# Attention and two mixture layers in one Trainium2 kernel: a new written order of the steps that hold both attention and the first layer's matmuls

## The chip, the cores and the metric

The kernel runs on one core of one Trainium2 chip. The metric is device time in microseconds (us), from several runs; one further execution was taken with the hardware profiler, and all rows of the trace come from that one. Engines are named as in the profile: PE (TensorE matmul), PEld (its weight load), DVE (VectorE), ACT (ScalarE), POOL (GpSimd), SP (SyncE, which here only issues DMAs).

## The reference, cut to what matters

```python
scores = scale * q @ k.T            # 4 batches, 8 heads, 576 positions, head size 64
scores += bias (ALiBi); causal window of 128
attn = softmax(scores) @ v          # -> x, 2304 tokens x 512
a, b = x @ w_a, x @ w_b             # 512 -> 1536
x = (a * b) @ w_out                 # 1536 -> 512
logits = x @ w_gate + modality_bias[modality_id]
e_idx = argmax(logits); gate_w = softmax(logits)[e_idx]      # 8 experts
out = gate_w * (relu(x @ w1[e_idx]) @ w2[e_idx])             # 512 -> 1024 -> 512
```

## The kernel before, in words

The 2304 tokens are 18 tiles of 128. They are worked in seven chunks of 3, 2, 2, 3, 3, 3 and 2 tiles (chunks 0 to 6). For each chunk there are twelve steps j, one for each block of 128 columns of w_a and w_b. The loop `for c ... for j` at L1149 calls `step0` for chunk 0 and `step` for chunks 1 to 5; chunk 6 has a loop body of its own (L1183 on).

**A step on PE.** `mm_ab(c, j, 0)` (12 matmuls, product "a"), `mm_ab(c, j, 1)` (product "b"), then pieces of attention, then `mm_out` (L539, L535), which adds the output product of the step before. Values are held as a high and a low half (type fp32r), so each product is three matmuls.

**Attention beside it.** One item is one query tile of a pair of heads. It takes three steps: in the first `score_mm` (PE), the mask and maximum on DVE (`score_sel`, `score_max`), `score_exp` on ACT; in the second the sum's inverse on DVE, `score_nrm` on ACT (L300), the transposes `pt_tr` on PE (L317) and `pt_cp`, which copies the high half on ACT (L330), subtracts the low half on DVE (L331) and masks twice on POOL into `pt` (L333, L335); in the third `a_pv`, the product with V ("PV", L401), two copies `u` out of PSUM on ACT (L408), two small DMAs to `z` and an addition on POOL; `z_add` adds `z` a step later. Items run ahead of their chunk: while chunk c is in its steps, attention of chunk c+1 is computed. `x_split` at the end of a chunk makes the next chunk's two halves `xr`. In `step` the list `sc` holds the items of the second stage, `tp` those of the third, `new` those that begin. In chunk 0 the PV of chunk 1's items goes through `pv_mm`, `pv_ev`, a transpose `pv_tr` (L369) and a copy `pv_x`.

**The gated product.** `gf` = a*b on DVE (L1102, needs the copy `asb` of a by ACT), its high half `g` on ACT (L1115), its low half on DVE (L1116). `mm_out` of the next step reads both; for the last step of a chunk `mm_out` stands right at the start of the next chunk.

**Routing.** `evac_out` copies a chunk's finished sums on ACT (L635) into tiles `x2`, of which there are three. For chunks 2 to 5 the logits are made on DVE (`rd_dot`, L620, one dot per tile and expert in steps 1 to 8), and then each tile has a generator in the list `ranks`: its first part is the argmax and the exponential, its second the gate value (`gate`, which also issues the DMA of `x2` to the table `x2d`, L580), the rank by two small matmuls, and a scatter. Before, the first part of at most two tiles runs in a step and the second part of one tile at the end of a step: for three tiles, the second parts end steps 9, 10 and 11. Chunks 0 and 1 go through `route` and the list `tr`.

**Output weights.** They come as float64 (`wo_load`, L484, into `wor`), are turned into float32 by three DVE instructions (`wo_jobs(j-1)` in step j of chunk 0, tile `f64o`) and written to DRAM as `wo_f` (L495). `wor`, `f64o` and the later `wo` share one tag "wo" with four buffers.

**What sets the order.** From chunk 0's steps to the end of chunk 5 the orders of PE, ACT and DVE are those of the program text (manual schedule); SP and POOL, and all of chunk 6, are ordered by the scheduler.

Of the kernel before, what the change touches and what calls it, by code (L numbers as in the profile page):

```python
# [16 lines left out]
P = 128  # L17
# [4 lines left out]
def attn_moe_moe2(ctx: ExitStack, tc, q, k, v, moe_w_a, moe_w_b, moe_w_out, modality_id,  # L22
# [33 lines left out]
    const = ctx.enter_context(tc.tile_pool(name="const", bufs=1))  # L56
    rt = ctx.enter_context(tc.tile_pool(name="rt", bufs=2))
    m1 = ctx.enter_context(tc.tile_pool(name="m1", bufs=2))
# [327 lines left out]
    def a_pv(it):  # L386
        a, t = it.a, it.t
        xf_new(a)
        if a.c in V32:
            pv_mm(it)  # L390
            pv_ev(it)
            pv_tr(it)
            pv_x(it, 0)
            return

        ps = ps_at.tile([P, 4, P], F32, tag="att", name="ps_o")
        for h in range(2):
            for b in range(2):  # L400
                nc.tensor.matmul(ps[:, 1 - h::2], lhsT=a.vv[:, t + b, h].rearrange("p r d -> p (r d)"),  # L401
                                 rhs=it.pt[:, h, b], start=(b == 0), stop=(b == 1))
        u = at.tile([P, 3, P], F32, tag="u", bufs=2, name="u")
        z = at.tile([P, P], F32, tag="z", bufs=2, name="z")
        n = slice(t * P, (t + 1) * P)
        for h in range(2):
            o = 64 * h
            nc.scalar.copy(out=u[o:o + 64], in_=ps[o:o + 64, 1 - h:4 - h])  # L408
# [3 lines left out]
        nc.gpsimd.tensor_tensor(out=xf_t[a.c, a.hp][:, n], in0=u[:, 0], in1=u[:, 2], op=ALU.add)  # L412
        zq.append(lambda: nc.gpsimd.tensor_tensor(out=xf_t[a.c, a.hp][:, n], in0=xf_t[a.c, a.hp][:, n],
                                                  in1=z, op=ALU.add))

    def z_add():
        for f in zq:
            if "pt" in mark:
                with tc.issue_after(mark["pt"]):
                    f()  # L420
            else:
                f()
        zq.clear()
# [140 lines left out]
    def route_fin(i, t, x2, pl, late=False):  # L564
# [20 lines left out]
        nc.vector.tensor_scalar(out=oh, in0=iot[:, 0:E], scalar1=sc[:, 2:3], scalar2=None, op0=ALU.is_equal)  # L585
        yield
        if t is None:
            pr = ps_at.tile([P, E], F32, tag="att", name="ps_r")
        else:
            pr = ps_acc.tile([P, E], F32, tag=f"acc{t}", name="ps_r")  # L590
        nc.tensor.matmul(pr, lhsT=tri, rhs=oh, start=True, stop=False)
        nc.tensor.matmul(pr, lhsT=ones, rhs=osum, start=False, stop=True)
        if late:
            gate()
        nc.vector.tensor_tensor(out=osum, in0=osum, in1=oh, op=ALU.add)
# [413 lines left out]
    def step0(j, pend, sc, tp):  # L1009

        n, last = CH[0] * P, j == NJ - 1
        new = list(range(cur["s"], goal[j]))
        its = [live[g] for g in tp]
        if j + 2 < NJ:
# [31 lines left out]
        for f in js[3:4]:  # L1046
            f()
        for it in its:
            pv_tr(it)
            pv_x(it, 0)  # L1050
        for g in new:
            score_red(live[g])
        if last:
            wo_fetch(0, 1)
            wo_fetch(1, 1)
            x_split(1)
        for g in new:
# [436 lines left out]
```

## Time and profile before

| | us |
|---|---|
| runs before, median (lowest to highest) of 3 | 854.33 (854.24 to 855.41) |
| the profiled execution, its own time | 853.42 |
| its span, first to last instruction | 851.4 |
| mean granted clock of PE in it | 0.988 |

The page of the profile gives the busy time of each engine over the span, then slices, the longest groups and the chain that ended last. Chunk 0's steps lie at about 46 to 142 us, chunk 1 to 219, chunk 2 to 295, chunk 3 to 380, chunk 4 to 473, chunk 5 to 560, chunk 6 to about 615; then come the experts. In a timeline row the first number is the start in us, the second the length; what stands in brackets at the end is the idle time of the engine just before and what ended it. A group of several instructions in one row ("x2") may hold short gaps.

### The profile page before, as it was taken

How to read it: one execution, taken by the hardware profiler on the slowest of the kernel's cores; microseconds unless marked ns; L12 is line 12 of the kernel's file. 1: busy time of each engine (PE TensorE's matmuls, PEld its weight loads, DVE VectorE, ACT ScalarE, POOL GpSimd, SP SyncE). 2: the span in 40 equal slices, each digit the busy share in tenths (PEclk: the TensorE clock that was granted, in tenths of full speed). 3: DMA queues.
4: the chain of work that ended last, by engine and by line, in shares of the span. 5: the costliest groups of instructions: out<-in, count | busy, mean ns of one | idle time of the engine just before them, and what ended most of it. 6: DMA issues, size and time to landing. Idle time of an engine off the chain costs nothing.

```text
span 851.4 us, 14429 instructions
## 1 busy us (share of the span) xinstructions
PE 810.0 (95%) x4726; PEld 727.2 (85%) x4726; DVE 541.2 (64%) x1559; ACT 458.4 (54%) x1149; POOL 230.1 (27%) x349
## 2 busy tenths in 40 slices
PE   7898999999999999999999899999999999999994
PEld 5876777898888899999999799988988998989893
DVE  7668887777666676667776667567575544448320
ACT  6743435777777776677666643322345443547420
POOL 5411000343234333352324322201132130114011
PEclk9899999999999999999999999999999999999998
DMA  8993325577556696554555444358438655448301
GB/s 242 370 388 105 105 95 176 178 210 225 178 145 169 167 218 165 152 149 141 164 148 154 105 131 127 106 150 269 132 122 284 222 174 154 149 143 289 122 32 39
DMA packets 77348, 144.60 MB, mean 170 GB/s; under 512 B 13839, under 2 KB 40623, under 8 KB 77264
## 3 DMA queue, kind: packets, MB, share of 16 engines
q1 hardware_dynamic: 73712, 133.86, 52.2%
q0 software_dynamic: 3552, 9.73, 3.1%
q8 instruction: 39, 0.64, 0.3%
q14 instruction: 45, 0.37, 0.1%
HBM read 118.16 MB, written 22.12 MB: 165 GB/s over the span
## 4 chain that ended last, share of the span: by engine, by line
PE 68%; ACT 8%; DMA 8%; DVE 7%; issue 6%; POOL 2%; SPq 1%; POOLq 0%; ACTq 0%; DVEq 0%
PE ps_ab L522 27%; PE acc L539 11%; PE ps_y L1230 9%; PE ps_h L1247 8%; PE acc L535 3%; PE ps_o L401 2%; DMA x2d<-x 2%; PE ps_s L253 2%; ACT u L408 2%; PE ps_p L317 1%; PE ps_o L356 1%; ACT p L277 1%; DVE g L1116 1%; DMA xg<-x2d,idx 1%; PE ps_t L970 1%
## 5 line engine op out<-in xcount | busy, mean ns | idle before, releaser
L522 PE MATMUL ps_ab<-xr,wab 128*128 128x384 f32 (+1 forms) x2016 | 323.8, 316 | 3.1 <-ACT asb L1196 1.6
L522 PEld LDWEIGHTS ps_ab<-xr,wab 128*128 128x128 f32 x2016 | 306.9, 188 | 12.8 <-issue 4.5
L539 PE MATMUL acc<-wo,g 128*128 128x512 f32 x540 | 138.7, 398 | 1.6 <-ACT g L1115 1.6
L333 POOL TENSOR_SCALAR_AFFINE_SELECT pt<-pc 128x512 fp32r<-128x512 f32 (+1 forms) x72 | 43.8, 608 | 305.1 <-DVE pc L331 217.6
L539 PEld LDWEIGHTS acc<-wo,g 128*128 128x128 f32 x540 | 97.7, 190 | 20.6 <-ACT g L1115 2.4
L1247 PE MATMUL ps_h<-xT,w1s 128*128 128x384 f32 x576 | 104.3, 337 | 0.0
L1230 PE MATMUL ps_y<-w2s,h 128*128 128x512 f32 x432 | 104.1, 394 | 0.0
L1247 PEld LDWEIGHTS ps_h<-xT,w1s 128*128 128x128 f32 x576 | 99.7, 188 | 1.4 <-issue 0.5
L1230 PEld LDWEIGHTS ps_y<-w2s,h 128*128 128x128 f32 x432 | 79.8, 188 | 15.8
L277 ACT ACTIVATE p<-p,mx 128x128 f32<-128x128 f32 x144 | 56.7, 395 | 48.5 <-DVE mx L267 48.1
L620 DVE CUSTOM_DVE_ANT_0 junk<-x,wgt 128x512 f32<-128x512 f32 x88 | 62.1, 705 | 8.3 <-DMA wgt<-in_wgt 3.6
L1116 DVE TENSOR_TENSOR g<-gf,g 128x384 fp32r<-128x384 f32 (+1 forms) x60 | 40.6, 676 | 33.3 <-ACT g L1115 32.9
L408 ACT COPY u<-ps_o 64x384 f32<-64x384 f32 x104 | 49.3, 474 | 9.4 <-PE ps_o L401 6.6
L921 DVE TENSOR_TENSOR w2s<-wr,w2s 128x1024 fp32r<-128x1024 f32 x24 | 29.4, 1225 | 38.3 <-ACT w2s L920 38.0
L1102 DVE TENSOR_TENSOR gf<-ps_ab,asb 128x384 f32<-128x384 f32 (+1 forms) x60 | 30.2, 503 | 36.5 <-PE ps_p L317 20.4
L1237 POOL DMA_INDIRECT out<-y,idx x18 | 21.5, 1194 | 113.6 <-ACT y L1236 111.8
L300 ACT ACTIVATE p<-p,mx 128x128 f32<-128x128 f32 x104 | 36.2, 395 | 24.8 <-DVE mx L285 24.6
L1250 ACT ACTIVATE h<-ps_h 128x384 fp32r<-128x384 f32 x48 | 23.5, 490 | 44.1 <-PE ps_h L1247 44.0
L921 DVE TENSOR_TENSOR w1s<-wr,w1s 128x1024 fp32r<-128x1024 f32 x28 | 34.3, 1224 | 20.4 <-ACT w1s L920 20.4
L335 POOL TENSOR_SCALAR_AFFINE_SELECT pt<-pc 128x512 fp32r<-128x512 f32 (+1 forms) x72 | 46.4, 645 | 0.0
L1251 DVE SCALAR_TENSOR_TENSOR h<-ps_h,h 128x384 fp32r<-128x384 f32 x48 | 26.4, 554 | 27.7 <-ACT h L1250 27.7
L317 PE MATMUL ps_p<-ident,p 128*128 128x128 f32 x144 | 32.3, 290 | 10.5 <-ACT p L300 10.0
(221 smaller groups left out, 1207.2 us busy)
## 6 DMA issues: line engine op xcount, KB each, us to landing
wo<-wo_d SPq DMA_DIRECT2D x60, 512.0 KB, 3.9
wr<-in_moe_w SPq DMA_DIRECT2D x56, 512.0 KB, 4.5
wgt<-in_wgt SPq DMA_DIRECT2D x32, 256.0 KB, 3.4
wraw<-in_moe_w_a SPq DMA_DIRECT2D x12, 512.0 KB, 8.6
wraw<-in_moe_w_b SPq DMA_DIRECT2D x12, 512.0 KB, 9.3
wor<-in_moe_w_out SPq DMA_DIRECT2D x12, 512.0 KB, 3.6
wo_d<-wo SPq DMA_DIRECT2D x12, 512.0 KB, 3.3
kr<-in_k SPq DMA_DIRECT2D x24, 256.0 KB, 4.0
```

What stands on the lines that cost most here:

```text
L277: nc.scalar.activation(out=it.p[:, h, :], in_=it.p[:, h, :], func=AF.Exp, bias=it.mx[:, 2 + h:3 + h], scale=-1.0, accum_out=it.mx[:, 4 + h ...
L317: nc.tensor.transpose(it.pp[:, h, :], it.p[:, h, :], ident)
L333: nc.gpsimd.affine_select(out=it.pt[:, :, 0], in_=pc, pattern=pat + [[-1, P]], base=0, channel_multiplier=1, compare_op=ALU.is_gt, fill=0.0)
L335: mark["pt"] = nc.gpsimd.affine_select(out=it.pt[:, :, 1], in_=pc, pattern=pat + [[1, P]], base=0, channel_multiplier=-1, compare_op=ALU.i ...
L408: nc.scalar.copy(out=u[o:o + 64], in_=ps[o:o + 64, 1 - h:4 - h])
L522: nc.tensor.matmul(ps[:, :n], lhsT=w[:, m, r, kk * P:(kk + 1) * P], rhs=xr[:, s, kk, :n], start=(idx == 0), stop=(idx == len(terms) - 1))
L539: nc.tensor.matmul(acc[c, t], lhsT=g[:, r, t * P:(t + 1) * P], rhs=w[:, s, :], start=(j == 0 and idx == 0), stop=(j == NJ - 1 and idx == 2))
L620: nc.vector.tensor_tensor_reduce(out=junk, in0=x2[:, 0:DM], in1=wgt[0][:, e % 2], scale=1.0, scalar=0.0, op0=ALU.mult, op1=ALU.add, accum_ ...
L921: nc.vector.tensor_tensor(out=dst[:, 1], in0=srcw, in1=dst[:, 0], op=ALU.subtract)
L1116: nc.vector.tensor_tensor(out=gt[:, 1, :n], in0=gf[:, :n], in1=gt[:, 0, :n], op=ALU.subtract)
L1230: nc.tensor.matmul(pss[t], lhsT=h[:, r, f, t * P:(t + 1) * P], rhs=W2[f // 2][:, s_, f % 2, :], start=(f == 0 and i == 0), stop=(f == 7 an ...
L1247: nc.tensor.matmul(ps, lhsT=W1[f // 2][:, r, kk, (f % 2) * P:(f % 2 + 1) * P], rhs=xT[:, s_, kk, :], start=(kk == 0 and i == 0), stop=(kk ...
```

## The change

(1) `rt` has three buffers instead of two. (2) `a_pv` now holds the PV matmuls alone, and the copies, DMAs and additions are a function `pv_out`; in `step`, PV stands right behind product b and ahead of `pt_tr`. (3) In `step`, `g`'s high half and low half stand right behind `gf`, ahead of `pt_cp` and of the copies `u` on ACT and ahead of L331 and `score_sel` on DVE. (4) In `step0` the items of the third stage have `pv_tr` and `pv_x` behind `mm_out`, and so have the last step's `wo_fetch` and `x_split(1)`; step 0 has no PV any more, step 1 does it for two items. (5) The late form of `route_fin` has its gate as a part of its own; in `step` all tiles of `ranks` take their first part in one step and their gate in the next, and one tile takes its last part at the end of a step from there on. (6) `wo_load(j)` is called in step j from step 1 on, in place of `wo_load(j+1)`. (7) A check that all `z` of a chunk are added before `x_split`.

```diff
-    rt = ctx.enter_context(tc.tile_pool(name="rt", bufs=2))
+    rt = ctx.enter_context(tc.tile_pool(name="rt", bufs=3))
...
     def a_pv(it):
         a, t = it.a, it.t
         xf_new(a)
...
-        ps = ps_at.tile([P, 4, P], F32, tag="att", name="ps_o")
+        it.po = ps_at.tile([P, 4, P], F32, tag="att", name="ps_o")
         for h in range(2):
             for b in range(2):
-                nc.tensor.matmul(ps[:, 1 - h::2], lhsT=a.vv[:, t + b, h].rearrange("p r d -> p (r d)"),
+                nc.tensor.matmul(it.po[:, 1 - h::2], lhsT=a.vv[:, t + b, h].rearrange("p r d -> p (r d)"),
                                  rhs=it.pt[:, h, b], start=(b == 0), stop=(b == 1))
+
+    def pv_out(it):
...
         yield
+        if late:
+            gate()
+            yield
         if t is None:
...
-        if late:
-            gate()
             pr = ps_at.tile([P, E], F32, tag="att", name="ps_r")
...
-        its = [live[g] for g in tp]
+        its = [live[g] for g in tp] if j else []
...
-        for it in its:
-            pv_tr(it)
-            pv_x(it, 0)
         for g in new:
             score_red(live[g])
-        if last:
-            wo_fetch(0, 1)
-            wo_fetch(1, 1)
-            x_split(1)
         for g in new:
             score_exp(live[g])
         new_preps(goal[j + 2], goal[j])
         if pend is not None:
             mm_out(*pend, wo_t[j - 1])
+        for it in its:
+            pv_tr(it)
+            pv_x(it, 0)
+        if last:
+            wo_fetch(0, 1)
+            wo_fetch(1, 1)
+            x_split(1)
...
-        return (0, j, gf), new, sc
+        return (0, j, gf), new, sc if j else tp + sc
...
-        for r in ranks[:2]:
-            if r[0] == 0:
+        for r in ranks:
+            if r[0] < 2:
                 next(r[1])
-                r[0] = 1
+                r[0] += 1
...
+        gt = m1.tile([P, 2, MT * P], F32R, tag="g", bufs=2, name="g")
+        nc.scalar.copy(out=gt[:, 0, :n], in_=gf[:, :n])
+        nc.vector.tensor_tensor(out=gt[:, 1, :n], in0=gf[:, :n], in1=gt[:, 0, :n], op=ALU.subtract)
+        for g in tp:
+            a_pv(live[g])
         for g in sc:
             pt_tr(live[g])
             pt_cp(live[g])
         z_add()
         for g in tp:
-            a_pv(live.pop(g))
+            pv_out(live.pop(g))
         for g in new:
             c_, hp_, t_ = items[g]
             live[g] = score_mm(pairs[c_, hp_], t_)
         for g in new[:1]:
             score_sel(live[g])
-        gt = m1.tile([P, 2, MT * P], F32R, tag="g", bufs=2, name="g")
-        nc.scalar.copy(out=gt[:, 0, :n], in_=gf[:, :n])
-        nc.vector.tensor_tensor(out=gt[:, 1, :n], in0=gf[:, :n], in1=gt[:, 0, :n], op=ALU.subtract)
...
-        if ranks and ranks[0][0] == 1:
+        if ranks and ranks[0][0] == 2:
             next(ranks.pop(0)[1], None)
...
-                if j + 1 < NJ:
-                    wo_load(j + 1)
+                if j:
+                    wo_load(j)
```

## Rows read from the trace of the kernel before

**Rows 1.** Windows: length; busy PE, PEld, DVE, ACT, POOL; granted clock, DMA, GB/s.

```profile
46.00:150.00 104.00, 97.46 (x485) 77.68 (x484) 82.93 (x159) 42.69 (x113) 11.83 (x20) 1.00 0.49 165
150.00:219.00 69.00, 65.28 (x471) 59.07 (x469) 49.40 (x165) 51.95 (x146) 26.45 (x41) 1.00 0.67 207
219.00:295.00 76.00, 71.30 (x507) 64.31 (x507) 48.44 (x166) 54.68 (x155) 28.46 (x49) 1.00 0.58 158
295.00:475.00 180.00, 180.00 (x1052) 168.99 (x1051) 130.72 (x440) 121.49 (x325) 65.08 (x103) 1.00 0.61 161
```

**Rows 2.** Waits of PE: us in total, times, longest.

```profile
PE ps_p L317 <- ACT p L300: 10.0, 11, 3.3
...
PE ps_o L369 <- ACT u L362: 1.9, 3, 0.7
...
PE acc L539 <- ACT g L1115: 1.6, 2, 1.0
```

**Rows 3.** Timeline of PE in chunk 0.

```profile
67.52 2.84 PE L535 MATMUL acc<-f64o,gf 128*128 128x512 f32 x6 [3.55 <-DVE f64o L446]
```

**Rows 4.** Timeline of DVE in chunk 0.

```profile
63.80 0.52 DVE L442 TENSOR_SCALAR f64o<-wor 128x512 uint32<-128x512 uint32 x1 [4.97 <-DMA wo_f<-f64o]
```

**Rows 5.** The page, DMA issues: size, median us to landing.

```profile
wor<-in_moe_w_out SPq DMA_DIRECT2D x12, 512.0 KB, 3.6
```

**Rows 6.** Timeline of PE in chunk 2, transposes of two steps.

```profile
227.75 0.62 PE L317 MATMUL ps_p<-ident,p 128*128 128x128 f32 x2 [0.28 <-ACT p L300]
...
289.75 0.62 PE L317 MATMUL ps_p<-ident,p 128*128 128x128 f32 x2 [0.19 <-ACT p L300]
```

**Rows 7.** Timeline of ACT in chunk 2, one step.

```profile
242.09 0.38 ACT L330 CAST pc<-ps_p 128x256 fp32r<-128x256 f32 x1
...
243.34 0.41 ACT L1115 CAST g<-gf 128x256 fp32r<-128x256 f32 x1
244.74 0.41 ACT L277 ACTIVATE p<-p,mx 128x128 f32<-128x128 f32 x1 [0.99 <-DVE mx L267]
```

**Rows 8.** Timeline of DVE in chunk 2, the same step.

```profile
242.49 0.42 DVE L331 TENSOR_TENSOR pc<-ps_p,pc 128x256 fp32r<-128x256 f32 x1 [0.26 <-ACT pc L330]
242.83 0.42 DVE L261 COPY_PREDICATED ps_s<-upper,ps_s 128x256 f32<-128x256 uint8 x1
243.78 0.71 DVE L1116 TENSOR_TENSOR g<-gf,g 128x256 fp32r<-128x256 f32 x1 [0.53 <-ACT g L1115]
```

**Rows 9.** Timelines of SP's queue and of ACT between chunks 4 and 5.

```profile
474.13 0.38 SPq L580 DMA_DIRECT2D x2d<-x  x1
...
480.37 0.59 ACT L635 COPY x<-acc 128x512 f32<-128x512 f32 x1 [3.11 <-DMA x2d<-x]
```

**Rows 10.** Timeline of PE, second step of chunk 5.

```profile
486.51 0.77 PE L317 MATMUL ps_p<-ident,p 128*128 128x128 f32 x2 [3.34 <-ACT p L300]
```

**Rows 11.** Windows, the same stretch: columns as in the first group.

```profile
486.00:493.00 7.00, 6.49 (x22) 5.51 (x23) 6.10 (x19) 4.46 (x13) 2.42 (x4) 0.53 0.16 48
```

**Rows 12.** Timelines of ACT and of PE at the start of chunk 6.

```profile
565.75 0.58 ACT L635 COPY x<-acc 128x512 f32<-128x512 f32 x1 [2.63 <-DMA x2d<-x]
...
566.66 3.12 PE L522 MATMUL ps_ab<-xr,wab 128*128 128x256 f32 x24 [1.59 <-ACT asb L1196]
```

**Rows 13.** Timelines of ACT, DVE and PE, a step of chunk 4.

```profile
406.25 0.70 ACT L300 ACTIVATE p<-p,mx 128x128 f32<-128x128 f32 x2 [0.50 <-DVE mx L285]
...
409.01 0.37 ACT L330 CAST pc<-ps_p 128x256 fp32r<-128x256 f32 x1 [1.04 <-PE ps_p L317]
...
410.44 0.51 ACT L1115 CAST g<-gf 128x384 fp32r<-128x384 f32 x1
...
409.57 0.55 DVE L1102 TENSOR_TENSOR gf<-ps_ab,asb 128x384 f32<-128x384 f32 x1
...
408.54 0.38 PE L317 MATMUL ps_p<-ident,p 128*128 128x128 f32 x2
408.68 0.72 PE L401 MATMUL ps_o<-pt,vv 128*128 128x256 f32 x4
```

More of the change, by code (lines that the diff above doesn't have):

```diff
@@ L388, in a_pv @@
         xf_new(a)
-        if a.c in V32:
-            pv_mm(it)
-            pv_ev(it)
-            pv_tr(it)
-            pv_x(it, 0)
-            return
-        ps = ps_at.tile([P, 4, P], F32, tag="att", name="ps_o")
+        it.po = ps_at.tile([P, 4, P], F32, tag="att", name="ps_o")
         for h in range(2):
             for b in range(2):
-                nc.tensor.matmul(ps[:, 1 - h::2], lhsT=a.vv[:, t + b, h].rearrange("p r d -> p (r d)"),
+                nc.tensor.matmul(it.po[:, 1 - h::2], lhsT=a.vv[:, t + b, h].rearrange("p r d -> p (r d)"),
                                  rhs=it.pt[:, h, b], start=(b == 0), stop=(b == 1))
+    def pv_out(it):
+        a, n = it.a, slice(it.t * P, (it.t + 1) * P)
         u = at.tile([P, 3, P], F32, tag="u", bufs=2, name="u")
         z = at.tile([P, P], F32, tag="z", bufs=2, name="z")
-        n = slice(t * P, (t + 1) * P)
         for h in range(2):
             o = 64 * h
-            nc.scalar.copy(out=u[o:o + 64], in_=ps[o:o + 64, 1 - h:4 - h])
+            nc.scalar.copy(out=u[o:o + 64], in_=it.po[o:o + 64, 1 - h:4 - h])
         for h in range(2):
@@ L411, in a_pv @@
             nc.sync.dma_start(out=z[o:o + 64], in_=u[d:d + 64, 1])
-        nc.gpsimd.tensor_tensor(out=xf_t[a.c, a.hp][:, n], in0=u[:, 0], in1=u[:, 2], op=ALU.add)
-        zq.append(lambda: nc.gpsimd.tensor_tensor(out=xf_t[a.c, a.hp][:, n], in0=xf_t[a.c, a.hp][:, n],
-                                                  in1=z, op=ALU.add))
+        xf = xf_t[a.c, a.hp][:, n]
+        nc.gpsimd.tensor_tensor(out=xf, in0=u[:, 0], in1=u[:, 2], op=ALU.add)
+        zq.append((a.c, lambda: nc.gpsimd.tensor_tensor(out=xf, in0=xf, in1=z, op=ALU.add)))
     def z_add():
-        for f in zq:
+        for _, f in zq:
             if "pt" in mark:
@@ L426, in x_split @@
         n = CH[c] * P
+        assert all(d > c for d, _ in zq)
         if c not in xr_t:
@@ L1047, in step0 @@
             f()
-        for it in its:
-            pv_tr(it)
-            pv_x(it, 0)
         for g in new:
             score_red(live[g])
-        if last:
-            wo_fetch(0, 1)
-            wo_fetch(1, 1)
-            x_split(1)
         for g in new:
@@ L1061, in step0 @@
             mm_out(*pend, wo_t[j - 1])
+        for it in its:
[5 more added lines that the diff above has]
+            x_split(1)
         cur["s"] = goal[j]
-        for g in tp:
+        for g in tp if j else ():
             live.pop(g)
-        return (0, j, gf), new, sc
+        return (0, j, gf), new, sc if j else tp + sc
     def step(c, j, pend, sc, tp):
@@ L1134, in step @@
             if tr[0][0] == 5:
-                tr.pop(0)
-        if ranks and ranks[0][0] == 1:
+                next(tr.pop(0)[1], None)
+        if ranks and ranks[0][0] == 2:
             next(ranks.pop(0)[1], None)
```

## The prediction

> **What bounds the kernel now.** I read the waits and windows first, then the timelines of the places that they point to. The windows show one engine at work nearly all the time: in the 180 us of chunks 3, 4 and the end of chunk 2 PE is busy for all 180.00 us, so nothing off PE can gain there. Idle time of PE lies in chunk 0's steps (104.00 - 97.46 = 6.54 us), in chunk 1 (3.72) and in chunk 2 (4.70) [rows 1]. The list of PE's waits names the transposes of `pt_tr`, held by the normalised `p` from ACT: 10.0 us in 11 waits, the longest 3.3; next to it the transposes of chunk 0 and the first `mm_out` behind a chunk's end [rows 2]. Three further stops are single ones: 3.55 us in chunk 0 [rows 3], 3.34 us in chunk 5 [rows 10], 1.59 us in chunk 6 [rows 12]. So the question for each edit is whether it removes one of these stops of PE, and what PE meets next.
>
> The sum below is made against the profiled execution's 853.42 us (span 851.4 and 2.0 around it). The median of the runs is 0.91 above it; I take the gain off the median.
>
> **The change part by part.**
>
> *Output weights one step later.* In step 2 DVE stood for 4.97 us until the DMA that writes `f64o` had freed a buffer [rows 4]; the four buffers of the tag held two or three `wor` loaded ahead. Loaded one step later, `wor` of block 0 is used up by then and its buffer is free, so DVE starts 4.97 us earlier. `mm_out`, which waited for DVE until 67.52, would have its weights at 67.52 - 4.97 = 62.55; PE was there at 67.52 - 3.55 = 63.97 [rows 3]. The whole 3.55 us go. Price: the load has one step less of lead. It lands in a median 3.6 us [rows 5], and a step of chunk 0 lasts about 104/12 = 8.7 us [rows 1], so it is hidden by that step; only the last block is used in the step that loads it, and there SP can send it as soon as a buffer is free, a step before. I count 0; at the worst DVE waits once for 3.6 us.
>
> *Order of step 0's pieces.* The transposes of PV wait for `u` from ACT: 1.9 us in 3 waits [rows 2]. Behind `mm_out`, whose six matmuls take 2.84 us [rows 3], ACT has ended first. The third of these waits and the waits for `pt` beside it lie in step 0, together 6.54 - 3.55 - 1.3 = 1.7 us; there PV is moved to step 1. But step 1's `mm_out` needs float32 weights from DVE, which comes no sooner, so I keep only 0.3 of the 1.7. Chunk 0: 3.55 + 1.3 + 0.3 = 5.1 us, bounds 3.5 and 6.5 (all idle time). The two-half split `x_split(1)` now stands behind these copies on ACT; the twelve matmuls of two `mm_out` in a row (about 2 x 2.6 us) cover it. If not, chunk 1 begins up to 0.5 us late.
>
> *PV ahead of the transposes, `g` ahead of `pt_cp`.* In chunk 2 the ten steps between the first and the last of these transposes took 62.00 us, 6.20 each [rows 6]. PE needs less: 4.70 us of idle time over twelve steps [rows 1], and in many pairs of transposes the second stood too: 0.62 us for a pair [rows 6] against 0.38 where nothing waits [rows 13]. That is about 0.5 us a step, so PE alone would need 5.7. What sets 6.20 is a ring of ACT and DVE: `pc` at 242.09, two copies `u`, `g` at 243.34, then DVE's low half of `g` at 243.78 for 0.71, the maximum, the exponential at 244.74 [rows 7, 8], the inverse, `p`, the transposes, and `pc` again. `pc` to exponential is 2.65 us. Written the new way it is, from the start of `g`: 0.41 for `g`, 0.71 for its low half, 0.42 each for `pc`'s low half and the selection [rows 7, 8] and 0.25 to the exponential (244.74 less 243.78 less 0.71), so 2.2; the copies of ACT fall into the time in which it waits for DVE. The ring gets 0.45 shorter, and PE's wait also shrinks by the PV that stands in front, about 0.6 of the 0.72 in the row [rows 13]. The ring then needs 5.75, PE 5.7; with steps that carry more on ACT I take 5.85: 0.35 x 11 = 3.9 us in chunk 2, bounds 1.6 (0.15 a step) and 5.3. Chunk 1 has nine items and 3.72 us of idle time: 2.4, bounds 1.2 and 3.5. At the ends of chunks 1 and 2 `mm_out` waited for `g`, 1.6 us in two waits [rows 2]; `g` now comes over 1 us sooner, but the split of `x` behind it becomes the next late thing: 1.2, bounds 0.5 and 2.
>
> [...]
>
> What is added: the first product now waits for `pt` straight behind b, one transpose pair sooner, and `pt` itself is made about a microsecond later, since `pc` is behind `g`. POOL has the rest of a step for it, 5.7 us in chunk 2, so it is hidden by the step's matmuls; in steps with preparations on ACT the cover ends. No row shows such a wait of chunk 2: 0 to 2.4 us (four steps of 0.6), I take 1.2.
>
> In 3-tile chunks PE was never idle, so `g` first costs nothing while its cover holds. A step of chunk 4: `p` is done at 406.95, PE comes at 408.54, a cover of 1.59, and PV adds 0.6 [rows 13]. `gf` ends at 410.12, `g` takes 0.51, so `pc` starts 1.6 us later than at 409.01 [rows 13], but the exponential, which has the same instructions ahead of it on DVE, only some 0.6 later. The DMAs to `z` move with `u`, and SP has nothing else due there.
>
> *Gates in one step.* The gate of the third tile stood at the end of step 11: its DMA was issued at 474.13, and ACT, copying the next sums into that buffer, waited 3.11 us and started at 480.37 [rows 9]; `pc`, `g` and `p` stood behind it on ACT, and PE waited 3.34 us at 486.51 [rows 10]. [...] With the gate at the start of step 10 the DMA, which took 480.37 - 474.13 = 6.2 us, has more than ten to land, even if three 256 KB writes share the queue. Gain 3.34 + 3.1 = 6.4, bounds 5 and 6.6. The same wait at the start of chunk 6 (2.63 on ACT, 1.59 on PE) [rows 12] goes too: 1.6, bounds -1 and 2.6, as the scheduler orders that chunk anew. Added: one more first part (about 1 us of DVE) in step 9 and two more gates in step 10, both under the cover of 1.6 to 2.2 above. The last tile's last part (two small matmuls and some short DVE work) falls into the next chunk.
>
> Sum: 5.1 + 3.9 + 2.4 + 1.2 - 1.2 + 6.4 + 1.6 = 19.4. 854.33 - 19.4 = **834.9 us**.
>
> **The rivals.**
>
> *The ring stays the bound in chunks 1 and 2.* ACT's preparations and the later `pt` take what the order gives; PV then waits for `pt` in place of the transposes for `p`. For it: ACT and DVE are busy for 55 and 48 of 76 us there, in a fixed order [rows 1]. Against it: the steps without preparations wait too. The 6.3 of that part (3.9 + 2.4 + 1.2 - 1.2) fall to 1: 840.2.
>
> *The stop in chunk 5 comes back in another shape*, since three writes at once delay what SP sends behind them, or another buffer is late. The 6.4 and 1.6 are lost: 842.9.
>
> *The load order does not change on the chip.* SP's order is not hand-written; if a later `wor` still takes the fourth buffer, the 3.55 stay: 838.5.
>
> *Slower: ACT held by `gf`.* In steps 1 to 8 of chunks 3 to 5 DVE makes dots before `gf`, and `g` now stands on ACT in front of `pc`, `u` and the exponential. The point is the cover: it decides from where the exponential comes more than 2.2 us later, instead of 0.6. [...] If the exponential came 3 us later, each of some 35 steps would lose 0.8, 28 us, against the 19.4: 862.9. The rows speak for 0.6.
>
> **How the numbers follow.** The forecast has 0.68, the ring 0.14, chunk 5 0.05, the load order 0.05, the slower case 0.05, and 0.03 is left for the gain going in something not seen, within 0.2%. A measurement of this kernel can tell about 0.2% (1.7 us) from no change. Faster is 0.68 + 0.14 + 0.05 + 0.05 = 0.92, same 0.03, slower 0.05. The forecast's own spread, with half of the bounds at once, is 830 to 840; the range goes on to 843 to take in the ring, the load order and chunk 5. Outside are the slower case, the unseen one and some of the forecast's tails.
>
> **What would show it.** Right: no wait of PE on `f64o` in chunk 0; transposes of chunk 2 about 5.85 us apart; no wait of ACT for the `x2d` DMA at the start of chunks 5 and 6, and a granted clock of 1.00 from 475 to 494's counterpart; the 180 us of chunks 3 and 4 unchanged. Wrong: a row of PE waiting for `pt` or `p` in chunks 3 to 5, PE waiting for POOL's `pt` in many steps of chunk 2, or a new low stretch of the clock.

## The result and the profile after

The changed kernel takes 828.72 us (median of four runs, 827.59 to 829.98), the kernel before 854.29 beside it (854.24 to 855.41): ratio 0.9698, 95% interval 0.9677 to 0.9719. It is 25.6 us faster. The forecast was 834.9 with a range from 830.0: the sign and the places were right, the size was 6 us too small, and the time lies 1.3 us below the range.

Windows of the changed kernel over chunk 0, chunk 1, chunk 2, the long stretch behind it, and the first two and a half steps of chunk 5 (columns as in [rows 1]):

```profile
44.00:143.00 99.00, 97.34 (x484) 77.72 (x483) 82.09 (x164) 42.84 (x115) 11.90 (x22) 1.00 0.53 178
143.00:209.00 66.00, 65.74 (x489) 61.34 (x487) 48.68 (x168) 52.66 (x149) 25.57 (x40) 1.00 0.71 220
209.00:279.00 70.00, 69.29 (x506) 64.27 (x505) 47.24 (x167) 54.10 (x154) 26.70 (x50) 1.00 0.62 172
279.00:457.00 178.00, 177.80 (x1037) 168.12 (x1038) 127.92 (x425) 117.77 (x325) 55.35 (x100) 1.00 0.61 162
457.00:476.00 19.00, 17.65 (x110) 17.16 (x109) 14.75 (x52) 11.36 (x32) 6.84 (x10) 1.00 0.47 129
```

In the window of chunk 1 PE now idles 0.26 us where it was 3.72, in that of chunk 2 0.71 where it was 4.70. (Cut at the chunks' own ends, as in the table below, it is 0.58 against 3.73 and 0.60 against 4.68.) The clock is at 1.00 through the start of chunk 5, where [rows 11] had a mean of 0.53. PE's waits agree:

```profile
PE ps_o L356 <- POOL pt L333: 3.6, 1, 3.6
PE ps_r L591 <- DVE pc L331: 1.3, 1, 1.3
...
PE ps_p L317 <- ACT p L300: 0.6, 2, 0.4
PE ps_o L369 <- ACT u L362: 0.6, 1, 0.6
```

The transposes' 10.0 us in 11 waits [rows 2] are 0.6 in 2. The first row is a stop in the start-up, ahead of chunk 0. The second is new and the largest of those that the change made: a small matmul of the ranks in chunk 5's first step. A smaller one is 0.92 us for `gf` in step 0 of chunk 0, where the kernel before waited 0.91 for `pt` and 0.61 for `u`.

To see where the 25.6 us come from I cut the span at the first copy `asb` of each chunk in ACT's timeline. Two of these cuts in the changed kernel, the ends of its chunks 1 and 2:

```profile
211.57 0.37 ACT L1081 COPY asb<-ps_ab 128x256 f32<-128x256 f32 x1 [2.07 <-PE ps_ab L519]
...
281.18 0.48 ACT L1081 COPY asb<-ps_ab 128x384 f32<-128x384 f32 x1
```

Chunk 2 thus is 281.18 - 211.57 = 69.61 us. The table has such lengths for all kernels of this study (us; "rest" runs from chunk 6's first copy to the end of the span).

| kernel | start | 0 | 1 | 2 | 3 | 4 | 5 | rest | span |
|---|---|---|---|---|---|---|---|---|---|
| before | 44.57 | 104.46 | 72.91 | 75.67 | 88.91 | 89.28 | 90.43 | 285.17 | 851.4 |
| after | 44.48 | 98.90 | 68.19 | 69.61 | 89.00 | 89.14 | 83.66 | 284.72 | 827.7 |
| e1, `g` late | 45.17 | 98.90 | 73.17 | 75.69 | 89.04 | 89.16 | 83.05 | 284.72 | 838.9 |
| e6, low half late | 43.56 | 98.90 | 71.26 | 74.28 | 89.14 | 91.61 | 83.49 | 282.96 | 835.2 |
| e2, transposes first | 45.31 | 98.89 | 68.80 | 69.72 | 88.82 | 88.84 | 83.63 | 284.29 | 828.3 |
| e3, gates one by one | 43.33 | 98.89 | 68.25 | 69.49 | 88.83 | 89.76 | 87.24 | 283.71 | 829.5 |
| e4, weights early | 43.59 | 102.60 | 68.47 | 69.57 | 89.15 | 89.15 | 83.66 | 285.21 | 831.4 |
| e5, step 0's old PV | 43.40 | 100.66 | 68.29 | 69.55 | 89.02 | 89.15 | 83.67 | 284.06 | 827.8 |
| e7, two last parts | 43.78 | 98.90 | 68.25 | 69.53 | 89.15 | 89.79 | 82.42 | 283.98 | 825.8 |
| e8, bias later | 44.30 | 98.91 | 68.30 | 69.57 | 89.11 | 89.15 | 83.66 | 284.50 | 827.5 |
| e9, two inputs more | 44.38 | 98.89 | 72.63 | 75.31 | 89.44 | 93.97 | 83.86 | 283.22 | 841.7 |
| e10, one input more | 44.67 | 98.89 | 71.24 | 73.72 | 89.18 | 91.76 | 83.79 | 282.65 | 835.9 |
| e13, PSUM input more | 44.35 | 98.89 | 71.22 | 73.40 | 89.08 | 91.39 | 83.64 | 284.43 | 836.4 |
| e11, `g`'s order alone | 44.37 | 104.41 | 68.76 | 69.88 | 88.87 | 89.74 | 87.48 | 286.99 | 840.5 |
| e12, gates alone | 44.34 | 103.29 | 72.99 | 75.71 | 88.64 | 88.89 | 83.02 | 285.22 | 842.1 |

The change takes 5.56 us from chunk 0, 4.72 and 6.06 from chunks 1 and 2, 0 from 3 and 4, 6.77 from chunk 5 and 0.45 behind it: 23.7 with the start. The other 1.9 us of the medians' difference are not a stage: the profiled execution of before was 0.9 below its median and that of after (829.83) 1.1 above its own. The columns "start" and "rest" move by up to 2 and 4 us between kernels that do the same there, so only columns 0 to 5 are read closely; even there e12's chunk 0 differs by 1.17 us with nothing changed in it.

One step of the changed kernel in chunk 2, beside [rows 7, 8] (timeline, all engines, lines of ACT, DVE and POOL):

```profile
236.52 0.41 ACT L1102 CAST g<-gf 128x256 fp32r<-128x256 f32 x1
...
236.83 0.38 ACT L330 CAST pc<-ps_p 128x256 fp32r<-128x256 f32 x1
236.97 0.42 DVE L1103 TENSOR_TENSOR g<-gf,g 128x256 fp32r<-128x256 f32 x1 [0.82 <-ACT g L1102]
...
237.31 0.42 DVE L331 TENSOR_TENSOR pc<-ps_p,pc 128x256 fp32r<-128x256 f32 x1
...
237.65 0.42 DVE L261 COPY_PREDICATED ps_s<-upper,ps_s 128x256 f32<-128x256 uint8 x1
...
237.80 0.64 POOL L333 TENSOR_SCALAR_AFFINE_SELECT pt<-pc 128x512 fp32r<-128x512 f32 x1 [3.63 <-DVE pc L331]
...
238.10 0.29 DVE L267 CUSTOM_DVE_ANT_0 p<-ps_s,m_base 128x128 f32<-128x128 f32 x1
...
238.44 0.40 ACT L277 ACTIVATE p<-p,mx 128x128 f32<-128x128 f32 x1 [0.36 <-DVE mx L267]
```

The low half (L1103) takes 0.42 us, not the 0.71 of [rows 8], and has ended before POOL's first selection (L333) begins. From `g` to the exponential it is 238.44 - 236.52 = 1.92 us; the prediction had 2.2. The transposes (PE's timeline, the first and the last of the ten steps measured in [rows 6]):

```profile
216.95 0.62 PE L317 MATMUL ps_p<-ident,p 128*128 128x128 f32 x2
...
274.66 0.38 PE L317 MATMUL ps_p<-ident,p 128*128 128x128 f32 x2
```

57.71 us for ten steps, 5.77 each, where it was 6.20. In chunk 0, PE and DVE at the place of [rows 3, 4]:

```profile
63.92 2.41 PE L532 MATMUL acc<-f64o,gf 128*128 128x512 f32 x5
```
```profile
60.51 0.42 DVE L439 TENSOR_SCALAR f64o<-wor 128x512 uint32<-128x512 uint32 x1
```

Neither waits. At the change from chunk 4 to chunk 5, SP's queue, ACT and PE (beside [rows 9, 10]):

```profile
445.05 1.54 SPq L577 DMA_DIRECT2D x2d<-x  x3
...
459.70 1.57 ACT L633 COPY x<-acc 128x512 f32<-128x512 f32 x3
...
463.68 0.17 PE L591 MATMUL ps_r<-oh,tri 128*128 128x8 bf16 x1 [1.35 <-DVE pc L331]
```

The three writes leave together, 14.7 us before ACT copies into the buffers, and ACT doesn't wait. What is late next is the third tile's small matmul L591: its PSUM buffer is one of those of the attention, and DVE frees it with `pc`.

### The profile page after: what moved, and what is told of

The parts are those of the page before. It is cut to its first block, busy times and chain, and to the rows that moved or that the text cites. A ratio compares the mean times of both kernels' runs of the same rounds, so it can differ in the third digit from the quotient of the medians.

```text
span 827.7 us, 14382 instructions
## 1 busy us (share of the span) xinstructions
PE 802.3 (97%) x4726; PEld 725.9 (88%) x4726; DVE 534.3 (65%) x1559; ACT 452.3 (55%) x1149; POOL 219.2 (26%) x349
## 4 chain that ended last, share of the span: by engine, by line
PE 68%; DVE 8%; issue 8%; ACT 7%; DMA 4%; POOL 2%; SPq 1%; POOLq 0%; ACTq 0%; DVEq 0%
PE ps_ab L519 30%; PE acc L536 11%; PE ps_h L1247 7%; PE ps_y L1230 6%; PE acc L532 4%; PE ps_o L395 2%; PE ps_s L253 2%; ACT p L277 1%; PE ps_p L317 1%; PE ps_o L356 1%; DMA wr<-in_moe_w 1%; PE ps_s L249 1%; DMA raw<-in_q 1%; DVE g L1103 1%; DVE p L267 1%
## 5 line engine op out<-in xcount | busy, mean ns | idle before, releaser
L536 PE MATMUL acc<-wo,g 128*128 128x512 f32 x540 | 136.2, 394 | 0.0
L333 POOL TENSOR_SCALAR_AFFINE_SELECT pt<-pc 128x512 fp32r<-128x512 f32 (+1 forms) x72 | 43.7, 608 | 323.6 <-DVE pc L331 234.9
L1102 ACT CAST g<-gf 128x384 fp32r<-128x384 f32 (+1 forms) x60 | 28.2, 471 | 49.1 <-DVE gf L1100 48.6
L1103 DVE TENSOR_TENSOR g<-gf,g 128x384 fp32r<-128x384 f32 (+1 forms) x60 | 30.4, 507 | 37.9 <-ACT g L1102 37.9
```

Of the source, the lines that this page charges most:

```text
L333: nc.gpsimd.affine_select(out=it.pt[:, :, 0], in_=pc, pattern=pat + [[-1, P]], base=0, channel_multiplier=1, compare_op=ALU.is_gt, fill=0.0)
L536: nc.tensor.matmul(acc[c, t], lhsT=g[:, r, t * P:(t + 1) * P], rhs=w[:, s, :], start=(j == 0 and idx == 0), stop=(j == NJ - 1 and idx == 2))
```

## The experiments

Each kernel was timed beside the kernel before on the same chip (medians of before 852.49 for e1, e2, e3 and e6, 854.17 for e4, e5, e7 and e8, 853.01 for e9 to e12, 852.96 for e13). The e1 to e10 and e13 edits are made to the changed kernel, e11 and e12 to the kernel before.

### e1 and e6: where `g` stands

e1 puts both halves of `g` back behind the selection and leaves PV in front; e6 puts back only the low half, on DVE:

```diff
# e1
-        gt = m1.tile([P, 2, MT * P], F32R, tag="g", bufs=2, name="g")
-        nc.scalar.copy(out=gt[:, 0, :n], in_=gf[:, :n])
-        nc.vector.tensor_tensor(out=gt[:, 1, :n], in0=gf[:, :n], in1=gt[:, 0, :n], op=ALU.subtract)
...
         for g in new[:1]:
             score_sel(live[g])
+        gt = m1.tile([P, 2, MT * P], F32R, tag="g", bufs=2, name="g")
+        nc.scalar.copy(out=gt[:, 0, :n], in_=gf[:, :n])
+        nc.vector.tensor_tensor(out=gt[:, 1, :n], in0=gf[:, :n], in1=gt[:, 0, :n], op=ALU.subtract)
# e6: the last of these three lines alone
```

> The changed kernel with one edit undone: in chunks 1 to 5 the two halves of the gated product stand again behind the transposes' copies and the copies u; PV stays ahead of the transposes. Theory A (in chunks 1 and 2 a ring of ACT and DVE set the pace, and the order of the gated product shortened it; PV's place is not part of that ring): chunks 1 and 2 go back to about 6.2 us a step, 6 to 10 us slower than the changed kernel, 835 to 839 us; PE waits again at its transposes, or at PV. Rival B (PE only needed other work in front of the transposes): within 2 us of the changed kernel, 828 to 831. Rival C (the gain of the order is all in the low half no longer running beside POOL's masks, 0.71 to 0.42 us): some 3 to 4 us slower, and as slow as the run in which only the low half is put back.

> The changed kernel with only the low half of the gated product (DVE) put back behind the selection; the high half stays early on ACT. Theory A: the ring grows by 0.2 us for the place and 0.3 for running beside POOL's masks (0.71 us for 256 columns in place of 0.42), to 5.9 against PE's 5.7 in steps with preparations: 1 to 4 us slower, 829 to 833. Rival C: all of what the run with both halves late loses, 3 us or more, is here too. If instead the low half stays at 0.42 us there, the masks were not what lengthened it.

e1: 838.58 us (837.06 to 841.01), ratio 0.9819 (0.9777 to 0.9860). e6: 838.56 (837.23 to 839.57), ratio 0.9828 (0.9787 to 0.9870). In e1 chunks 1 and 2 are as long as before the change (73.17 and 75.69): without the place of `g`, PV in front of the transposes brings nothing. e6 shows that an early high half helps little while the low half stays: it loses 3.07 and 4.67 us in these chunks, so it keeps 1.65 of 4.72 and 1.39 of 6.06, and it loses 2.47 more in chunk 4, where nothing had been gained. In total it is as slow as e1, so the 1 to 4 us of its theory were too little and its rival came true in the total. A step of e6 in chunk 2 (timeline, DVE and POOL):

```profile
240.85 0.42 DVE L261 COPY_PREDICATED ps_s<-upper,ps_s 128x256 f32<-128x256 uint8 x1
...
241.01 0.64 POOL L333 TENSOR_SCALAR_AFFINE_SELECT pt<-pc 128x512 fp32r<-128x512 f32 x1 [3.95 <-DVE pc L331]
241.18 0.74 DVE L1116 TENSOR_TENSOR g<-gf,g 128x256 fp32r<-128x256 f32 x1
...
241.61 0.82 POOL L335 TENSOR_SCALAR_AFFINE_SELECT pt<-pc 128x512 fp32r<-128x512 f32 x1
241.85 0.28 DVE L267 CUSTOM_DVE_ANT_0 p<-ps_s,m_base 128x128 f32<-128x128 f32 x1
```

From the selection L261 to the first maximum L267 it is 1.00 us, against 238.10 - 237.65 = 0.45 in the changed kernel. The low half, which takes 0.42 alone, lies on POOL's two selections and takes 0.74, and POOL's second one takes 0.82.

### e9, e10 and e13: is it the place, or the company of POOL?

All three keep the changed order and add one VectorE instruction in the old place of the low half, whose result nothing reads:

```diff
         for g in new[:1]:
             score_sel(live[g])
+        # e9
+        nc.vector.tensor_tensor(out=gf[:, :n], in0=gf[:, :n], in1=gt[:, 0, :n], op=ALU.subtract)
+        # e10
+        nc.vector.tensor_scalar(out=gf[:, :n], in0=gf[:, :n], scalar1=2.0, scalar2=None, op0=ALU.mult)
+        # e13
+        for g in new[:1]:
+            nc.vector.tensor_scalar(out=gf[:, :n], in0=live[g].ps.rearrange("p a b -> p (a b)")[:, :n],
+                                    scalar1=2.0, scalar2=None, op0=ALU.mult)
```

> The changed kernel with one more VectorE instruction in every step of chunks 1 to 6, in the place that the low half of g had before (behind the triangle's copy into the scores): gf becomes gf minus g's high half, two operands from SBUF, and nothing reads the new gf. Theory: in that place it lies beside POOL's selections on pt and takes 0.70 to 0.75 us instead of 0.42, all of it in the ring of chunks 1 and 2, so these two chunks lose what the late low half cost: +6 to +10 us against 828.7, with the steps of chunks 3 and 4 as they were or a little longer. Rival: it is the wait of acc for the late half that costs, not VectorE's time: under +3.

> The same, but the added instruction has one operand from SBUF (gf becomes gf times two). Theory of the two operands: it takes the same time beside POOL's selections as alone, 0.3 to 0.42 us, and the loss is about half of the other's: +2.5 to +5 us. Rival 1: any VectorE instruction is slowed by POOL's selections there: 0.7 us and +6 to +10. Rival 2: the ring takes it up in its slack: under +1.

> The changed kernel with one more VectorE instruction in the same place as in the two runs with an added instruction, of the same width, but its one operand comes from PSUM (gf becomes the scores times two; nothing reads it). Theory: an instruction that reads PSUM is not slowed by POOL's selections, so it takes 0.42 us at 256 columns and 0.55 at 384. From those two runs chunk 2 has lost 4.1 us with 0.61 and 5.7 with 0.74, so about 0.27 us a step is free there and 0.42 should cost some 1.8 us in chunk 2 and a little less in chunk 1, with about 1 in chunk 4: +3.5 to +5 us against 828.7 (832 to 834). Rival 1: it is slowed as the others are, 0.74 and 0.88 us: +13 to +16. Rival 2: what costs is any added instruction, whatever its length: +8 to +10.

| | us (lowest to highest) | ratio to before (95%) | L261 to L267 | chunk 2 |
|---|---|---|---|---|
| after | 828.72 (827.59 to 829.98) | 0.9698 (0.9677 to 0.9719) | 0.45 | 69.61 |
| e13 | 838.05 (836.56 to 838.64) | 0.9818 (0.9797 to 0.9838) | 0.80 | 73.40 |
| e10 | 838.07 (837.95 to 838.92) | 0.9825 (0.9798 to 0.9852) | 0.86 | 73.72 |
| e9 | 844.16 (842.89 to 844.59) | 0.9892 (0.9863 to 0.9920) | 0.99 | 75.31 |

The durations are in the groups of the line list (ns: least, median, most; the least of e9 and of e10 are from steps in which POOL made no selection beside it), e9, e10 and e13 in turn:

```profile
L1117 DVE TENSOR_TENSOR gf<-gf,g x60: 414/746/882, 146.5 to 553.5; 128x384 f32<-128x384 f32 x36, 128x256 f32<-128x256 f32 x24
```
```profile
L1117 DVE TENSOR_SCALAR gf<-gf x60: 281/614/686, 146.7 to 548.4; 128x384 f32<-128x384 f32 x36, 128x256 f32<-128x256 f32 x24
```
```profile
L1118 DVE TENSOR_SCALAR gf<-ps_s x50: 423/557/558, 146.6 to 520.8; 128x384 f32<-128x384 f32 x29, 128x256 f32<-128x256 f32 x21
```

And e10's step in the timeline, for the overlap:

```profile
242.03 0.42 DVE L261 COPY_PREDICATED ps_s<-upper,ps_s 128x256 f32<-128x256 uint8 x1
242.19 0.64 POOL L333 TENSOR_SCALAR_AFFINE_SELECT pt<-pc 128x512 fp32r<-128x512 f32 x1 [4.02 <-DVE pc L331]
242.36 0.61 DVE L1117 TENSOR_SCALAR gf<-gf 128x256 f32<-128x256 f32 x1
...
242.78 0.68 POOL L335 TENSOR_SCALAR_AFFINE_SELECT pt<-pc 128x512 fp32r<-128x512 f32 x1
242.89 0.28 DVE L267 CUSTOM_DVE_ANT_0 p<-ps_s,m_base 128x128 f32<-128x128 f32 x1
```

The theory for e10 falls and its first rival comes true (9.4 us slower than the changed kernel): one operand from SBUF is slowed too, 0.28 to 0.61. The instruction that reads PSUM is not: 0.42 in all its steps of chunk 2, beside the same selections. But the theory for e13 falls as well, in its price: I had concluded from e9 and e10 that some 0.27 us a step were free. They aren't. Read by what reaches the ring, the time from L261 to L267, the added 0.35, 0.41 and 0.54 us cost 3.8, 4.1 and 5.7 us in chunk 2, which is 0.32, 0.34 and 0.48 in each of its twelve steps. So after the change the ring stands right at the edge: whatever VectorE gets in this place is paid nearly in full. e13's other rival, that any added instruction costs 8 to 10 us whatever its length, has the number right (9.3), but e9's longer one costs 6 us more.

How much of this is the place, and how much POOL's company, can be read from a step of e9 in which POOL makes no selection there (its first of chunk 2; POOL's only work beside it is an addition):

```profile
218.55 0.42 DVE L261 COPY_PREDICATED ps_s<-upper,ps_s 128x256 f32<-128x256 uint8 x1
...
218.88 0.42 DVE L1117 TENSOR_TENSOR gf<-gf,g 128x256 f32<-128x256 f32 x1
...
219.22 0.28 DVE L267 CUSTOM_DVE_ANT_0 p<-ps_s,m_base 128x128 f32<-128x128 f32 x1
```

From L261 to L267 it is 0.67 us: the place adds 0.22 to the 0.45 of the changed kernel, and POOL's selections bring this to 0.54. For e10 the same two are 0.08 (0.53 in such a step) and 0.41. So of what reaches the ring more than half is POOL's company. e13 cannot stand for the place alone: its instruction begins 0.45 us after L261, not 0.33; it reads the scores that L261 writes, so I take the difference for a wait. What the place without the company would cost in the whole chunk no run shows.

In chunk 4 the three cost 2.25, 2.62 and 4.83 us, though PE is busy there for nearly all of the time (177.80 of 178.00 us in the changed kernel's window of chunks 3 and 4). e9 is thus 15.4 us slower than the changed kernel, where 6 to 10 were expected: chunks 1 and 2 give 10.1 of it, chunk 4 most of the rest. A row of ACT in e6's chunk 4 shows how:

```profile
417.00 0.51 ACT L1102 CAST g<-gf 128x384 fp32r<-128x384 f32 x1 [1.29 <-DVE gf L1100]
```

ACT waits here for `gf`, which on DVE stands behind three dots of the routing, and `pc` behind it on ACT, and the selection and the exponential behind `pc`. The changed kernel has the same wait (1.53 us at 422.48), so the wait is not itself the loss; what differs is how long `p` lies ready before PE comes for it. ACT's and PE's rows of one step, the changed kernel first, then e6:

```profile
419.01 0.70 ACT L300 ACTIVATE p<-p,mx 128x128 f32<-128x128 f32 x2 [0.49 <-DVE mx L285]
...
422.10 0.38 PE L317 MATMUL ps_p<-ident,p 128*128 128x128 f32 x2
```
```profile
421.04 0.70 ACT L300 ACTIVATE p<-p,mx 128x128 f32<-128x128 f32 x2 [0.55 <-DVE mx L285]
...
421.78 0.38 PE L317 MATMUL ps_p<-ident,p 128*128 128x128 f32 x2
```

From the end of `p` to the transposes it is 2.39 us in the changed kernel and 0.04 in e6. In e6 there is nearly no slack left in this circle. The prediction's slower rival is this very mechanism.

### e11: the order of `g` alone, in the kernel before

The three lines of `g` (L1114 to L1116 there) are moved right behind `gf`, as in e1's diff the other way; nothing else.

> The kernel before with the order of g alone changed: both its halves right behind gf, everything else as before. Theory: the low half at 0.42 us out of VectorE's place behind the selection gives chunks 1 and 2 nearly all of their gain: -9 to -11 us, 843 to 845.5. Rival (the gain needs the PV's new order too): -3 to -6.

841.59 us (838.03 to 843.63), ratio 0.9854 (0.9814 to 0.9893): -11.4. Chunks 1 and 2 give 4.15 and 5.79 of the whole change's 4.72 and 6.06; chunk 5 gives 2.95, as its stop is shorter too. The gain in chunks 1 and 2 does not need PV's new order.

### e2: transposes ahead of PV again

```diff
-        for g in tp:
-            a_pv(live[g])
         for g in sc:
             pt_tr(live[g])
             pt_cp(live[g])
         z_add()
+        for g in tp:
+            a_pv(live[g])
```

> The changed kernel with the transposes again ahead of PV on PE, the gated product's halves still straight behind it. Theory A: the ring stays short (about 5.4 us against PE's 5.7), so the pace stays near PE's; transposes wait now and then where ACT has preparations: 0.5 to 3 us slower than the changed kernel, 829 to 832. Rival B: the 10 us of waits at the transposes return, 836 to 840.

830.40 us (828.55 to 830.44), ratio 0.9722 (0.9680 to 0.9763). Chunk 1 is 0.61 us longer, chunk 2 0.11. With `g` in front, PV's place is worth 0.7 us there; the intervals of e2 and of the changed kernel overlap.

### e3 and e12: the gates

e3 gives the changed kernel the old gates and ranks; e12 gives the kernel before the new ones:

```diff
-        for r in ranks:
-            if r[0] < 2:
+        for r in ranks[:2]:
+            if r[0] == 0:
                 next(r[1])
-                r[0] += 1
+                r[0] = 1
# e3; with it gate() back behind the two matmuls, and the last parts of tr and ranks as before. e12 is the reverse, with bufs=3 of rt.
```

> The changed kernel with the routing order of before: one gate at the end of each of three steps. Theory: ACT waits again for the last tile's DMA at the start of chunks 5 and 6; PE stands about 3.3 us in the second step of chunk 5, and the clock granted falls to half behind it for some 7 us (another 3 us); chunk 6 loses 1.6. The wait of 1.35 us that the changed kernel has at the rank's small matmul in chunk 5 goes. 6 to 8 us slower than the changed kernel, 835 to 837. Rival (the shift of chunks 1 to 4 alone removed that collision): no wait for that DMA, within 1 us of the changed kernel.

> The kernel before with the gates and the ranks of the chunk's tiles as changed (with a third set of their small buffers), everything else as before. [...] Rival: the gain is as large as what undoing it in the changed kernel cost, -2.5 to -3.5.

e3: 831.81 us (831.58 to 832.37), ratio 0.9747 (0.9707 to 0.9787), +3.1, where 6 to 8 were expected; its interval overlaps that of the changed kernel, so the reading rests on chunk 5, which is 3.58 us longer. e12: 844.23 (843.40 to 848.46), ratio 0.9904 (0.9870 to 0.9938), -8.8 (the author's estimate was -5 to -7.5), of which chunk 5 gives 7.41 and chunk 0, where nothing was changed, 1.17 (PE's wait for `f64o` is 2.4 us in this run instead of 3.5; why is open). So the stop is worth 7.4 us in the kernel before and less behind the rest of the change, since `g`'s order already shortened it (2.2 us of PE in e11, and e11's chunk 5 is as long as e3's): PE's longest waits at this place of e3 are

```profile
466.06 0.38 PE L395 MATMUL ps_o<-pt,vv 128*128 128x256 f32 x1 [0.59 <-POOL pt L333]
...
467.82 0.77 PE L317 MATMUL ps_p<-ident,p 128*128 128x128 f32 x2 [0.56 <-ACT p L300]
```

and the clock's mean over the 8 us from 466 to 474 is 0.79, where over the 7 us of [rows 11] it was 0.53.

### e4 and e5: chunk 0

```diff
# e4
-                if j:
-                    wo_load(j)
+                if j + 1 < NJ:
+                    wo_load(j + 1)
# e5: in step0; the last step's wo_fetch and x_split(1) go back up with these lines
-        its = [live[g] for g in tp] if j else []
+        its = [live[g] for g in tp]
...
+        for it in its:
+            pv_tr(it)
+            pv_x(it, 0)
         for g in new:
             score_red(live[g])
```

> The changed kernel with the fetches of the next block of output weights put back to their old place, a step earlier, everything else as changed. Theory (prediction's chunk 0 term): the loads take the DMA engines from f64o again, TensorE's first product of chunk 0 waits 3 to 3.6 us for it, and the time goes up by 3 to 4 us against the changed kernel (831.7 to 832.7 beside 828.7). Rival 1: the other edits have moved f64o's own load, the wait doesn't return and the time is within 1 us of 828.7. Rival 2: the loads that come a step earlier save waits later and it is faster by 1 us or more.

> The changed kernel with the first step's PV order put back (transposes and PV ahead of the reductions and of the products of output weights in step 0 of chunk 0 too). Theory: the wait of TensorE for u (1.9 us in 3 before the change) comes back in part, +0.5 to +2 us against 828.7. Rival: that wait lies beside the start-up, which DMA sets: within 0.5 us.

e4: 832.66 us (831.73 to 833.85), ratio 0.9747 (0.9728 to 0.9767), chunk 0 longer by 3.70. The wait is back with its cause, on PE and on DVE:

```profile
66.74 2.84 PE L532 MATMUL acc<-f64o,gf 128*128 128x512 f32 x6 [3.59 <-DVE f64o L443]
```
```profile
63.11 0.43 DVE L439 TENSOR_SCALAR f64o<-wor 128x512 uint32<-128x512 uint32 x1 [3.39 <-DMA wo_f<-f64o]
```

What DVE waits for is the buffer that the write of `wo_f` holds. The expectation put it on the DMA engines' time; the row bears out the prediction's wording, not that. e5: 830.66 (829.39 to 833.04), ratio 0.9733 (0.9709 to 0.9758), chunk 0 longer by 1.76 (the intervals of e5 and of the changed kernel overlap; the column and the waits carry the reading), with PE's waits for `u` back at

```profile
PE ps_o L369 <- ACT u L362: 1.9, 3, 0.7
```

### e7 and e8: what could still go

```diff
# e7
-        if ranks and ranks[0][0] == 2:
-            next(ranks.pop(0)[1], None)
+        for _ in range(2):
+            if ranks and ranks[0][0] == 2:
+                next(ranks.pop(0)[1], None)
# e8: constants of the bias, 5 places later in the start-up
-    CJ = 3
+    CJ = 8
```

> The changed kernel, but the end of a step runs up to two last parts of the ranks instead of one. Theory: the new wait of 1.35 us of TensorE at the start of chunk 5 (its small product of the ranks waits for pc of the attention that shares the buffers) goes, since the ranks are done a step earlier: -0.8 to -1.5 us against 828.7, with chunk 5's first steps 1.3 shorter. Rival: the wait only moves to the step before, or the extra gathers on POOL's queue delay the rows of chunk 5: 0 to +1.

> The changed kernel with the constants of the bias loaded five steps later in the start-up. [...]

e7: 828.72 us (827.82 to 829.90), ratio 0.9708 (0.9690 to 0.9725). The new wait is gone and chunk 5 1.24 us shorter; chunk 4, whose eleventh step now makes two of these parts, is 0.65 longer. Of the expected 0.8 to 1.5 us the runs show nothing. e8: 829.06 (827.66 to 829.57), ratio 0.9702 (0.9684 to 0.9720). The stop of 3.6 us in the start-up goes, another of 2.0 us for the same product comes at 31, and of the 3.5 to 6 us that were the author's estimate nothing is gained; windows over 15 to 30 and 30 to 44 us, the changed kernel first, then e8:

```profile
15.00:30.00 15.00, 11.27 (x60) 9.61 (x60) 8.16 (x33) 9.65 (x38) 6.95 (x14) 0.77 1.01 316
30.00:44.00 14.00, 12.95 (x88) 11.43 (x88) 11.43 (x43) 10.93 (x47) 6.75 (x15) 1.00 0.99 367
```
```profile
15.00:30.00 15.00, 14.36 (x97) 11.96 (x97) 12.76 (x58) 14.49 (x58) 7.08 (x19) 1.00 1.04 327
30.00:44.00 14.00, 11.96 (x53) 11.24 (x52) 7.42 (x20) 6.27 (x26) 5.68 (x11) 0.63 0.98 363
```

PE does more before 30 us and less behind it, at a lower clock, and chunk 0 begins at 44.30 instead of 44.48. The DMA column is at 0.98 to 1.04 in both: I read this as the loads setting this time, so that a wait of PE under them costs nothing; no run here changes the loads.

## Why the prediction was right and where it was wrong

**Chunk 0: right.** 5.1 was forecast, 5.56 measured; undone one by one, the load order costs 3.70 (3.55 forecast) and the order of step 0 1.76 (1.6 forecast).

**Chunks 1 and 2: the step that failed.** The four terms 3.9 + 2.4 + 1.2 - 1.2 = 6.3 measured 4.72 + 6.06 = 10.8. These 4.5 us are as much as the whole error in the profiled executions (19.4 against 23.7). Each term was too small:

- *The low half at 0.71.* It takes 0.42 in its new place. The forecast had both durations in its rows, 0.71 for the low half and 0.42 for two instructions of the same width ahead of it [rows 8], and kept the longer. With it from `g` to the exponential 1.92 us instead of 2.2, and the steps of chunk 2 are 5.77 us apart, not 5.85: 0.43 x 11 = 4.7 in place of 3.9. By the forecast's own sum the ring would then need 5.46 (5.75 less 0.29), less than the 5.7 that it gave PE, so that PE sets the pace again. The traces show the low half at 0.42 where POOL makes no selection beside it (the changed kernel's step above) and at 0.74 beside the selections (e6's step), so a sum with 0.42 would have been the better one.
- *Chunk 1, 2.4.* From its first transposes to its last (ten pairs) it is 60.98 us after 65.15: 4.2. The bound of 3.5 was about the idle time of PE in the window; but the transposes of the chunk, too, fell from 5.16 to 4.20 us in all, since six of their rows were of 0.53 us and more before, and two are now, where a pair that waits for nothing takes 0.38.
- *The ends, 1.2.* From the last transposes of chunk 1 to the first of chunk 2 it was 12.69 us and is 11.10, at the next end 9.52 and 8.60: 2.5. The split of `x` is the next late thing, as said, but PE waits for it only 0.5 us in all.
- *The new wait for `pt`, -1.2.* There is none in chunks 1 and 2. POOL begins at 237.80 in the rows above, its two selections take 0.64 each, and PV of the next step stands at 241.65.

That it is the place of the low half and not PV's is shown both ways: e1 loses all of the gain, e6 7.7 of the 10.8, e11 alone has 9.9 of it, and e2 keeps all but 0.7.

**Chunks 3 and 4: right in the sum (0 forecast, 0.05 measured), wrong in the margin.** The slower rival was given 0.05 with a cover of 2.2 us for the exponential, of which 0.6 was to be used. e13, e10 and e9 show it nearer: in chunk 4 the time from L261 to L267 grows from 0.45 to 0.93, 0.93 and 1.13 us, and a step by 0.19, 0.22 and 0.40, so only 0.26 to 0.29 us of cover are left, by all three alike. Chunk 3 has more: there the same three cost 0.08, 0.18 and 0.44 us in the whole chunk. Had the low half stayed behind the selection, the rival would have come true in small, as it does in e6 with 2.5 us in chunk 4.

**Chunk 5: right in kind, a little too large.** 6.4 and 1.6 were forecast. The first three steps (26.07 us before, from the `asb` copies) take 21.18: 4.9. The last, which ends at chunk 6's first copy, 8.60 after 10.29: 1.7. Of the 6.4, 3.34 is the stop of [rows 10]; the other 3.1 no run shows by itself. What the traces show is a mean clock of 0.53 over 486 to 493 before [rows 11] and of 1.00 over 457 to 476 after, and 4.9 us gained in all. The rival "comes back in another shape" came true in small: 1.35 us of PE at the ranks' matmul. Without the rest of the change (e12) the gain in chunk 5 is 7.4.

**Range.** It ended at 830.0 since I took half of the bounds at once. Chunks 1 and 2 measured 10.8 where their bounds at best gave 5.3 + 3.5 + 2 - 0 = 10.8, all four at the upper end together: they weren't independent, but all hung on one ring. The 1.3 us below the range are less than the 1.9 us that lie in no stage: with the 23.7 of the profiled executions alone the time would have been 830.6. That it came out just below the range is thus partly the scatter of the runs; that chunks 1 and 2 were sized too small is not.

## What to carry to other kernels

When engines take turns in a ring, price an instruction by what it adds between its two neighbours in the ring, and ask what runs beside it in its new place: its duration is not its own (the low half took 0.42 us alone and 0.74 beside POOL's selections). A bound on a moved wait should be taken for the whole ring at once, since the terms that hang on it rise and fall together. An engine at 100% busy in one stage does not mean that other queues there have room: chunk 4 had 0.3 us a step.

## What the runs showed that I had not expected

Beside POOL's selections the added or moved VectorE instruction on SBUF operands grows by about the same 0.33 us whether it has two (0.42 to 0.74, e6) or one (0.28 to 0.61, e10), at 256 columns; the one that reads PSUM stays at 0.42 (e13). POOL's second selection grows from 0.64 to 0.82 behind the first of these (e6, e9) and to 0.68 behind the second (e10), and stays at 0.64 behind the one that reads PSUM (e13). The delay goes the other way in a step of e6's chunk 1 in which VectorE came first: there it keeps its 0.41, and POOL's selection takes 0.75 instead of 0.64. What on the chip makes the one delay the other no run shows.

```profile
164.48 0.41 DVE L1116 TENSOR_TENSOR g<-gf,g 128x256 fp32r<-128x256 f32 x1
164.64 0.75 POOL L333 TENSOR_SCALAR_AFFINE_SELECT pt<-pc 128x512 fp32r<-128x512 f32 x1 [1.31 <-DVE pc L331]
```

The half-clock stretch of the start-up (0.50 from 22 to 28 us in the changed kernel, behind the stop of 3.6) did not go away with that stop: in e8 the clock's mean is 1.00 over 15 to 30 us, and the low stretch (a mean of 0.63 over 30 to 44) comes later, where PE stands for 2.04 us until 32.85. In e8 the stop was taken away, and the clock that had followed it was not won back.
